# Attention followed by a gated feed-forward: k and v with nine tokens of two heads per partition, k-z-v in 64-row halves, the norm weight by a product, wo queued behind the weights

## The chip, the cores and the metric

The kernel runs on one core of a Trainium2 chip. The metric is the device time of one execution in microseconds (us); medians, ranges and clocks come from several executions. The profile is of one execution, recorded by the hardware profiler: for the kernel before a further one, elsewhere one of those timed. Engines in it: PE is TensorE's matmuls, PEld its weight loads, DVE is VectorE, ACT is ScalarE, POOL is GpSimd, SP is SyncE. Matmul ends are modelled, so I read their starts.

## The reference

```python
# q, k, v: 8 batches x 8 heads x 576 tokens x 64, float32
def phi(x, c, s):
    r = np.maximum(x, 0.0)
    return np.concatenate([r * c, r * s], axis=-1)          # 64 -> 128 features
q_p, k_p = phi(q, cos_w, sin_w), phi(k, cos_w, sin_w)       # angle = pi/2 * token / 576
kv  = np.einsum('bhsf,bhsd->bhfd', k_p, v)
z   = np.sum(k_p, axis=2)
num = np.einsum('bhsf,bhfd->bhsd', q_p, kv)
den = np.einsum('bhsf,bhf->bhs', q_p, z)[..., None] + 1e-06
x   = (num / den)                                           # then 4608 rows of 512
xn  = x / np.sqrt(np.mean(x * x, -1, keepdims=True) + 1e-06) * rms_g
g, val = xn @ w_gate, xn @ w_val                            # 512 -> 1536
out = (silu(g) * val) @ w_out                               # 1536 -> 512
```

The product of phi(k) with v, and with a column of ones for z, is called k-z-v here. It is needed once in each batch.

## The kernel before

Each batch has 576 tokens. Before, 512 of them lie four to a partition, and a tail of 64 is loaded and cast apart. A head's k-z-v is five matmuls of 128 rows that accumulate.

```python
def load_main(which, src, b, heads=(0, 8), bufs=one, queue=nc.sync):
    ...
        in_=src[b, h0:h1, 0:512, :].rearrange("h (p j) d -> p h (j d)", j=4),
...
def kvz_pe(b, pst, heads=range(8)):
    o = headview(pst)
    for h in heads:
        for c in range(5):
            lhsT = kp_main[b][:, c, h, :] if c < 4 else kpt[b % 2][:, h % 4, :]
            rhs = vvm[b % 2][:, c, h, :] if c < 4 else vvt[b % 2][:, h, :]
            nc.tensor.matmul(o[:, h // 4, h % 4, :], lhsT=lhsT, rhs=rhs,
                             start=(c == 0), stop=(c == 4))
```

The opening keeps TensorE busy with matmuls on a tile of zeros ("fillers") until the first data is there. `V` and `A` are VectorE and ScalarE; `q_tr_pe` is a transpose of phi(q) on TensorE, and `q_tr_evac` is its copy out.

```python
nc.sync.dma_start(out=gb[:, :], in_=moe_rms_g ... .to_broadcast([P, DM]))   # norm weight
...
filler(31, idle)
...                                 # phi(k) of batch 0
for c in (0, 1):
    q_phi(V, 0, c, 0)
    q_phi(A, 0, c, 1)
q_tr_pe(0, 0, psV[0][:, :])
filler(2, idle)
q_tr_evac(V, 0, 0, psV[0][:, :])
q_tr_pe(0, 1, psO[0][:, :])
filler(4, idle)
...                                 # k-z-v of batch 0
```

At the joint, k-z-v of batch 1 and the transposes of its q stand between the output matmuls of block 0.

```python
for n in range(NNT - 2):
    if n == 0:
        ...                         # phi(q) of batch 1, second half
    if n == 3:
        kvz_pe(1, psA)
        ...
    if 1 <= n <= 4:
        c = n - 1
        q_tr_pe(1, c, qbank[c])
        q_tr_evac(V if c < 2 else A, 1, c, qbank[c])
    if n == 2:
        v_cast(A, 1, LOW)
        v_cast(V, 1, HIGH)
    ...
    for j in range(4):
        out_mm(0, j, n, banks0[j])
```

Of the kernel before, what the change touches and what calls it, by code (L numbers as in the profile page):

```python
# [13 lines left out]
SYNC_DEP = mybir.DependencyInfo(mybir.DependencyClass.Sync, mybir.DependencyReason.DATA)  # L14

# [7 lines left out]
def kernel(  # L23
# [40 lines left out]
    LOW, HIGH = (0, 4), (4, 8)  # L64
# [4 lines left out]
    def load_main(which, src, b, heads=(0, 8), bufs=one, queue=nc.sync):  # L69
        key = (which, b)  # L70
        if key not in raw:
            raw[key] = bufs.tile([P, H, 4 * D], FP32, name=f"r{which}", tag=f"r{which}")
        h0, h1 = heads
        return queue.dma_start(
            out=raw[key][:, h0:h1, :],
            in_=src[b, h0:h1, 0:512, :].rearrange("h (p j) d -> p h (j d)", j=4),
        )

    def load_tail(which, src, b, queue=nc.sync):
        t = (four if which == "q" else two).tile(  # L80
            [P, 4, D], FP32, name=f"r{which}t", tag=f"r{which}t"
        )
        raw[(which + "t", b)] = t
        for g in range(2):
            d = queue.dma_start(
                out=t[64 * g : 64 * g + 64, :, :],
                in_=src[b, 4 * g : 4 * g + 4, 512:576, :].rearrange("h s d -> s h d"),
            )
        return d

    src_of = {"k": k, "q": q, "v": v}
    last_load = {}

    def load_piece(which, b, p):
        if p < 4:
            load_main(
                which, src_of[which], b, (2 * p, 2 * p + 2), two if which == "k" else one
            )
        else:
            load_tail(which, src_of[which], b)  # L100

    def load(which, b):
        load_main(which, src_of[which], b, bufs=two if which == "k" else one)
        last_load[(which, b)] = load_tail(which, src_of[which], b)

    def load_tokens(which, b, j0, j1):

        key = (which, b)
        if key not in raw:
            raw[key] = one.tile([P, H, 4 * D], FP32, name=f"r{which}", tag=f"r{which}")  # L110
        view = src_of[which][b, :, 0:512, :].rearrange("h (p j) d -> p h j d", j=4)
        return nc.sync.dma_start(
            out=raw[key][:, :, j0 * D : j1 * D],
            in_=view[:, :, j0:j1, :].rearrange("p h j d -> p h (j d)"),
        )

    first = {}
    load_main("k", k, 0, LOW, two)
    load_tail("v", v, 0, A)
    load_main("k", k, 0, HIGH, two)  # L120
    load_tail("k", k, 0, A)
    load_tokens("q", 0, 0, 2)
    first["v"] = load_main("v", v, 0, LOW)
    load_main("v", v, 0, (4, 7))
    load_main("v", v, 0, (7, 8))
    load_tokens("q", 0, 2, 4)
    nc.scalar.preload_act_table(AF.Silu)

    gb = one.tile([P, DM], FP32, name="gb")
    with nc.allow_non_contiguous_dma(reason="rms_g to all partitions"):  # L130
        nc.sync.dma_start(
            out=gb[:, :],
            in_=moe_rms_g.rearrange("(o d) -> o d", o=1).to_broadcast([P, DM]),
        )


    iota_i = one.tile([P, 2], mybir.dt.int32, name="iota_i")
    nc.gpsimd.iota(iota_i[:, :], pattern=[[0, 2]], base=0, channel_multiplier=1)
# [7 lines left out]
    fidx = one.tile([P, 1], FP32, name="fidx")  # L146
    th = one.tile([P, 10], FP32, name="th")
    tab = one.tile([P, 10], FP32, name="tab")
    ang = math.pi / 2.0 / float(S)
    nc.vector.tensor_copy(out=fidx[:, :], in_=iota_i[:, 0:1])  # L150
    for j in range(4):
        nc.vector.tensor_scalar(
            out=th[:, j : j + 1], in0=fidx[:, :], scalar1=4.0 * ang, scalar2=j * ang,
            op0=ALU.mult, op1=ALU.add,
        )
    nc.vector.tensor_scalar(
        out=th[0:64, 4:5], in0=fidx[0:64, :], scalar1=512.0, scalar2=ang,
        op0=ALU.add, op1=ALU.mult,
    )
    nc.vector.tensor_scalar(  # L160
        out=th[64:128, 4:5], in0=fidx[64:128, :], scalar1=448.0, scalar2=ang,
        op0=ALU.add, op1=ALU.mult,
    )
    nc.vector.tensor_scalar(
        out=th[:, 5:10], in0=th[:, 0:5], scalar1=math.pi / 2.0, scalar2=math.pi,
# [4 lines left out]
    def sin_of(c, lo=0, hi=P):  # L170
        return tab[lo:hi, c : c + 1]

    def cos_of(c, lo=0, hi=P):
        return tab[lo:hi, 5 + c : 6 + c]
# [5 lines left out]
    kpt = [one.tile([P, 4, F], BF16, name=f"kpt{i}") for i in range(2)]  # L180
    vvt = [one.tile([P, H, E], BF16, name=f"vvt{i}") for i in range(2)]
    vvm = [one.tile([P, 4, H, E], BF16, name=f"vvm{i}") for i in range(2)]
# [3 lines left out]
    for i in range(2):  # L186
        nc.gpsimd.memset(vvt[i][64:128, 0:4, :], 0.0)
        nc.gpsimd.memset(vvt[i][0:64, 4:8, :], 0.0)
        nc.gpsimd.memset(vvt[i][0:64, 0:4, D:E], 1.0)
        nc.gpsimd.memset(vvt[i][64:128, 4:8, D:E], 1.0)  # L190
        nc.gpsimd.memset(vvm[i][:, :, :, D:E], 1.0)
# [16 lines left out]
    def view4(t, heads):  # L208
        return t[:, heads[0] : heads[1], :].rearrange("p h (j d) -> p h j d", d=D)
# [9 lines left out]
    def k_phi(eng, b, c, part, heads=(0, 8)):  # L219

        o = slice(0, D) if part == 0 else slice(D, F)
        f = cos_of if part == 0 else sin_of
        if c < 4:
            if b not in kp_main:
                kp_main[b] = one.tile([P, 4, H, F], BF16, name="kpm", tag="kpm")
            src = view4(raw[("k", b)], heads)[:, :, c, :]
            phi(eng, kp_main[b][:, c, heads[0] : heads[1], o], src, f(c))
        else:
            phi(eng, kpt[b % 2][:, :, o], raw[("kt", b)][:, :, :], f(4))

    def q_phi(eng, b, c, part, heads=(0, 8)):
# [6 lines left out]
        t = qp_tiles[(b, c)]  # L238
        if c < 4:
            src = view4(raw[("q", b)], heads)[:, :, c, :]  # L240
            phi(eng, t[:, heads[0] : heads[1], o], src, f(c))
        else:
            phi(eng, t[:, :, o], raw[("qt", b)][:, :, :], f(4))
# [32 lines left out]
    def v_cast(eng, b, heads=(0, 8)):  # L276
        copy(
            eng,
            vvm[b % 2][:, :, heads[0] : heads[1], 0:D],
            view4(raw[("v", b)], heads).rearrange("p h j d -> p j h d"),  # L280
        )

    def v_cast_tail(eng, b):
        for g in range(2):
            copy(
                eng,
                vvt[b % 2][64 * g : 64 * g + 64, 4 * g : 4 * g + 4, 0:D],
                raw[("vt", b)][64 * g : 64 * g + 64, :, :],
            )
# [4 lines left out]
    def kvz_pe(b, pst, heads=range(8)):  # L294
        o = headview(pst)
        for h in heads:
            for c in range(5):
                lhsT = kp_main[b][:, c, h, :] if c < 4 else kpt[b % 2][:, h % 4, :]
                rhs = vvm[b % 2][:, c, h, :] if c < 4 else vvt[b % 2][:, h, :]
                nc.tensor.matmul(  # L300
                    o[:, h // 4, h % 4, :], lhsT=lhsT, rhs=rhs, start=(c == 0), stop=(c == 4)
                )

    def kvz_evac(eng, b, pst, bank):
        kvzs[(b, bank)] = three.tile([P, 4 * E], BF16, name="kvzs", tag=f"kvzs{bank}")
        copy(eng, kvzs[(b, bank)][:, :], pst[:, bank, 0 : 4 * E])

    def kvz_half(b, view, heads):
        o = view[:, 0, 0 : 4 * E].rearrange("p (h e) -> p h e", e=E)
        for h in heads:  # L310
            for c in range(5):
                lhsT = kp_main[b][:, c, h, :] if c < 4 else kpt[b % 2][:, h % 4, :]
                rhs = vvm[b % 2][:, c, h, :] if c < 4 else vvt[b % 2][:, h, :]
                nc.tensor.matmul(
                    o[:, h % 4, :], lhsT=lhsT, rhs=rhs, start=(c == 0), stop=(c == 4)
                )

    def kvz_half_evac(eng, b, view, bank):
        kvzs[(b, bank)] = three.tile([P, 4 * E], BF16, name="kvzs", tag=f"kvzs{bank}")
        copy(eng, kvzs[(b, bank)][:, :], view[:, 0, 0 : 4 * E])  # L320

    def nd_pe(b, j, pst):

        o = headview(pst)
        for h in range(H):
            g, i = h // 4, h % 4
            if j < 4:
                nc.tensor.matmul(  # L328
                    o[:, g, i, :], lhsT=qpT[(b, 0)][:, h, j * P : (j + 1) * P],
                    rhs=kvzs[(b, g)][:, i * E : (i + 1) * E], start=True, stop=True,  # L330
                )
            else:
                for bb in (b - 1, b):
# [4 lines left out]
                        rhs=kvzs[(bb, g)][:, i * E : (i + 1) * E], start=True, stop=True,  # L338
                    )

    def nd_half(b, j, g, bank):
        o = bank[:, 0 : 4 * E].rearrange("p (h e) -> p h e", e=E)
        for i in range(4):
            nc.tensor.matmul(
                o[:, i, :], lhsT=qpT[(b, 0)][:, 4 * g + i, j * P : (j + 1) * P],
                rhs=kvzs[(b, g)][:, i * E : (i + 1) * E], start=True, stop=True,
# [142 lines left out]
    filler(31, idle)  # L489
    for heads in (LOW, HIGH):  # L490
        for c in range(4):
            k_phi(V, 0, c, 0, heads)
            k_phi(A if heads is LOW or c < 2 else V, 0, c, 1, heads)
# [377 lines left out]
```

## Time and profile before

| | before |
|---|---|
| time, three runs | 329.54 us median (328.85 to 329.59) |
| TensorE busy | 320.2 us, 98% of the span |
| VectorE, ScalarE, GpSimd busy | 55%, 51%, 12% |
| k-z-v of a batch in TensorE's chain | 1.21 us (1.29 in batch 1) |
| first q transpose / k-z-v of batch 0 starts | 10.96 / 13.15 us |
| first 512-column gate product of block 0 starts | 32.15 us |
| k-z-v of batch 1 starts | 46.66 us |

The way to read it: TensorE bounds the kernel, so a change counts only where it alters TensorE's own work or a moment at which TensorE waits. The starts in the table are those of the first matmul of the kind. The chain of waits dates the same groups 0.16 us later, because there a piece begins only where the piece before it is taken to end; so 46.82 in the prediction and 46.66 here are the same matmul.

### The profile page before, as it was taken

The numbers are of one execution on the slowest core, as the hardware profiler recorded it, in microseconds if no ns is written. First come the engines' busy times: TensorE is split into PE (matmuls) and PEld (weight loads), VectorE is DVE, ScalarE is ACT, GpSimd is POOL, SyncE is SP. The second block draws the span as 40 slices with busy tenths as digits, with TensorE's granted clock in tenths as the row PEclk, the third lists the DMA queues.
The fourth block names the chain that finished last, engine by engine and source line by source line (L and its number), as shares of the span: only waits on it lengthen the run. The fifth ranks groups of instructions, "written<-read, shape, count | busy, mean of one in ns | idle before, by whom it ended". The sixth has DMA issues, their size and how long they took to land.

```text
span 327.8 us, 5943 instructions
## 1 busy us (share of the span) xinstructions
PE 320.2 (98%) x2189; PEld 163.3 (50%) x2189; DVE 181.6 (55%) x376; ACT 168.5 (51%) x326; POOL 37.8 (12%) x83
## 2 busy tenths in 40 slices
PE   8999999999999999999999999999999999999995
PEld 3568455654445444544454445444544444444443
DVE  3775667777745775677257745772577134203410
ACT  4565665876646556545664566455644233223321
POOL 3520032001200112012001120120011000000000
PEclk9999999999999999999999999999999999999999
DMA  7999999999599988967698669866621400020014
GB/s 208 280 196 250 275 214 270 304 223 209 133 249 220 174 209 242 224 173 166 208 181 213 170 190 181 218 172 208 135 55 32 130 33 0 19 111 0 0 34 97
DMA packets 95117, 54.14 MB, mean 165 GB/s; under 512 B 60016, under 2 KB 90480, under 8 KB 95088
## 3 DMA queue, kind: packets, MB, share of 16 engines
q1 hardware_dynamic: 89072, 48.65, 59.3%
q0 software_dynamic: 4768, 4.72, 8.9%
q10 hardware_dynamic: 1248, 0.39, 0.6%
q8 instruction: 17, 0.28, 0.4%
q14 instruction: 12, 0.10, 0.1%
HBM read 38.01 MB, written 9.44 MB: 145 GB/s over the span
## 4 chain that ended last, share of the span: by engine, by line
PE 93%; DMA 3%; DVE 2%; issue 1%; ACT 0%; SPq 0%; DVEq 0%
PE psG L444 27%; PE psV L444 27%; PE psC L464 26%; PE psA L300 3%; DMA rq<-in_q_dram 3%; PE psA L328 2%; PE psG L464 1%; PE psG L569 1%; PE psV L569 1%; PE psO L569 1%; PE psV L263 1%; PE psG L484 1%; PE psO L263 1%; PE psA L335 0%; PE psG L831 0%
## 5 line engine op out<-in xcount | busy, mean ns | idle before, releaser
L459 DVE TENSOR_TENSOR hT<-psV,sg 128x512 bf16<-128x512 f32 x102 | 70.4, 690 | 97.7 <-PE psV L444 86.3
L453 ACT ACTIVATE sg<-psG 128x512 f32<-128x512 f32 x102 | 60.6, 594 | 66.3 <-PE psG L444 66.2
L444 PE MATMUL psG<-xnT,wg 128*128 128x512 bf16 (+1 forms) x368 | 92.8, 374 | 0.2
L444 PE MATMUL psV<-xnT,wv 128*128 128x512 bf16 (+1 forms) x368 | 92.8, 375 | 0.0
L464 PE MATMUL psC<-wo,hT 128*128 128x512 bf16 x396 | 89.6, 379 | 0.0
L444 PEld LDWEIGHTS <-wv 128*128 128x128 bf16 x416 | 40.6, 98 | 47.4
L464 PEld LDWEIGHTS <-hT 128*128 128x128 bf16 x420 | 40.1, 98 | 46.5
L444 PEld LDWEIGHTS <-wg 128*128 128x128 bf16 x416 | 38.5, 97 | 41.4 <-issue 0.6
L272 ACT COPY osb<-psC 128x512 f32<-128x512 f32 (+1 forms) x33 | 19.1, 578 | 44.3 <-PE psC L464 43.6
L398 POOL TENSOR_TENSOR rs<-ms,mhalf 128x1 f32<-128x1 f32 x36 | 19.8, 549 | 184.6 <-ACT scr L393 184.6
L405 DVE SCALAR_TENSOR_TENSOR xn<-xt,rs,gb 128x512 bf16<-128x512 f32 x36 | 27.3, 757 | 14.1 <-POOL rs L398 14.0
L393 ACT ACTIVATE scr<-xt 128x513 bf16<-128x513 f32 x36 | 22.8, 635 | 23.4 <-DVE xt L382 22.5
L382 DVE TENSOR_TENSOR xt<-psA,rec 128x512 f32<-128x512 f32 x35 | 24.2, 691 | 1.2
L213 ACT ACTIVATE qp<-rq,tab 128x512 bf16<-128x512 f32 x32 | 22.3, 713 | 3.6 <-DMA rq<-in_q_dram 3.6
L213 ACT ACTIVATE kpm<-rk,tab 128x512 bf16<-128x512 f32 (+1 forms) x34 | 21.2, 675 | 0.5 <-DMA rk<-in_k_dram 0.5
L215 DVE TENSOR_SCALAR kpm<-rk,tab 128x512 bf16<-128x512 f32 (+1 forms) x38 | 15.3, 455 | 4.3 <-ACT tab L168 3.3
L215 DVE TENSOR_SCALAR qp<-rq,tab 128x512 bf16<-128x512 f32 x32 | 15.0, 480 | 2.5 <-DMA rq<-in_q_dram 2.5
L484 PE MATMUL psG<-warm 128*128 128x512 bf16 x49 | 14.1, 434 | 1.2 <-DVE fidx L150 1.2
L328 PEld LDWEIGHTS <-qpT 128*128 128x128 bf16 x248 | 11.7, 98 | 6.8 <-DMA qpT<-qp 0.5
L328 PE MATMUL psA<-kvzs,qpT 128*128 128x65 bf16 x248 | 12.9, 194 | 0.2
L444 PE MATMUL psV<-xnt_tail,wv 128*128 128x512 bf16 x48 | 12.3, 379 | 0.0
L444 PE MATMUL psG<-xnt_tail,wg 128*128 128x512 bf16 x48 | 12.3, 379 | 0.0
(95 smaller groups left out, 194.5 us busy)
## 6 DMA issues: line engine op xcount, KB each, us to landing
out_dram<-osb SPq DMA_DIRECT2D x32, 256.0 KB, 2.6
rk<-in_k_dram SPq DMA_DIRECT2D x20, 256.0 KB, 3.8
rv<-in_v_dram SPq DMA_DIRECT2D x20, 256.0 KB, 3.1
rq<-in_q_dram SPq DMA_DIRECT2D x20, 256.0 KB, 3.2
rk<-in_k_dram SPq DMA_DIRECT2D x2, 1024.0 KB, 8.7
rq<-in_q_dram SPq DMA_DIRECT2D x2, 1024.0 KB, 11.0
rv<-in_v_dram SPq DMA_DIRECT2D x3, 512.0 KB, 10.8
wo<-in_moe_w_out_dram POOLq DMA_DIRECT2D x4, 384.0 KB, 7.7
```

The lines of the kernel that those rows point to most:

```text
L213: nc.scalar.activation(out=out_ap, in_=in_ap, func=AF.Relu, scale=scale)
L215: eng.tensor_scalar(out=out_ap, in0=in_ap, scalar1=scale, scalar2=0.0, op0=ALU.mult, op1=ALU.max)
L272: nc.scalar.copy(out=o, in_=i)
L328: nc.tensor.matmul(o[:, g, i, :], lhsT=qpT[(b, 0)][:, h, j * P : (j + 1) * P], rhs=kvzs[(b, g)][:, i * E : (i + 1) * E], start=True, stop= ...
L382: nc.vector.tensor_tensor(out=xt[:, 0:DM].rearrange("p (b h d) -> p b h d", b=2, d=D), in0=o[:, :, :, 0:D], in1=rec[:, :, :].unsqueeze(3). ...
L393: nc.scalar.activation(out=scr[:, :], in_=xt[:, 0 : DM + 1], func=AF.Square, scale=1.0 / math.sqrt(DM), accum_out=ms[:, :],)
L398: nc.gpsimd.tensor_tensor(out=rs[:, :], in0=ms[:, :], in1=mhalf[:, :], op=ALU.pow)
L405: nc.vector.scalar_tensor_tensor(out=xn[:, :], in0=x_of[(b, j)][:, 0:DM], scalar=rs_of[(b, j)][:, :], in1=gb[:, :], op0=ALU.mult, op1=ALU. ...
L444: nc.tensor.matmul(pst[bank][:, cols[0] : cols[1]], lhsT=w[:, t, n * P : (n + 1) * P], rhs=x[:, t, cols[0] : cols[1]], start=(t == 0), sto ...
L453: nc.scalar.activation(out=sg[:, :], in_=psG[bank][:, :], func=AF.Silu)
L459: nc.vector.tensor_tensor(out=hTs[blk][:, n, :], in0=psV[bank][:, :], in1=sg[:, :], op=ALU.mult)
L464: nc.tensor.matmul(bank, lhsT=hTs[blk][:, n, j * P : (j + 1) * P], rhs=wo[:, n, :], start=(n == 0), stop=(n == NNT - 1),)
```

## The change

It is meant to do four things. First, k and v are loaded in runs of 2304 bytes, nine tokens to a partition, with two heads in the two halves of the partitions; the tails of k and v go. Second, k-z-v then contracts over 64 rows, in nine steps for each head, with the two heads in turn, so that the halves of the array may work side by side. Third, the norm weight is spread over the partitions by a one-row product, and not by a broadcast load. Fourth, wo's first slice is queued directly behind the other weights, and the transposes of the joint are begun one step earlier.

```diff
+            in_=src[b, 2 * r0 : 2 * r1, :, :]
+            .rearrange("h s d -> (h s d)")
+            .rearrange("(r p n) -> p r n", p=P, n=NJ * D),
...
+    def kvz_mm(b, banks, rs=(0, 4)):
+        for r in range(*rs):
+            for j in range(NJ):
+                for c in range(2):
+                    lo = 64 * c
+                    nc.tensor.matmul(
+                        banks[c][:, r * E : (r + 1) * E],
+                        lhsT=kp_main[b][lo : lo + 64, j, r, :],
+                        rhs=vvm[b % 2][lo : lo + 64, r, j, :],
+                        start=(j == 0), stop=(j == NJ - 1),
+                    )
...
-    filler(31, idle)
+    filler(30, idle)
...
+    wo_load(0)
...
     q_tr_pe(0, 0, psV[0][:, :])
-    filler(2, idle)
     q_tr_evac(V, 0, 0, psV[0][:, :])
+    nc.tensor.matmul(psO[1][:, :], lhsT=ones[:, :], rhs=g_row[:, :], start=True, stop=True)
     q_tr_pe(0, 1, psO[0][:, :])
-    filler(4, idle)
+    filler(1, idle)
...
     for n in range(NNT - 2):
+        if n == 3:
+            kvz_pe(1, psA)
...
+        if n in (0, 1, 2, 4):
+            c = min(n, 3)
+            q_tr_pe(1, c, qbank[c])
+            q_tr_evac(V if c < 2 else A, 1, c, qbank[c])
         if n == 0:
...
+        if n == 2:
+            v_cast(A, 1, *LOW)
+            v_cast(V, 1, *HIGH)
         if n == 3:
-            kvz_pe(1, psA)
...
-        if 1 <= n <= 4:
-            c = n - 1
...
-        if n == 2:
-            v_cast(A, 1, LOW)
-            v_cast(V, 1, HIGH)
```

## The prediction

> **What bounds the kernel now.** I read the page first: which engine is full, then whether the chain agrees.
>
> ```profile
> PE 320.2 (98%) x2189; PEld 163.3 (50%) x2189; DVE 181.6 (55%) x376; ACT 168.5 (51%) x326; POOL 37.8 (12%) x83
> ...
> PE 93%; DMA 3%; DVE 2%; issue 1%; ACT 0%; SPq 0%; DVEq 0%
> ```
>
> TensorE is 98% busy and 93% of the chain that ended last is TensorE work. VectorE and ScalarE are half idle, so work moved between them costs nothing where they keep up. I then went through the starts of the matmuls in the trace and listed every place where the next start comes later than the stream's pace (216 ns at 512 columns, 30 ns at 65). From 62 us to the end there are only two waits, 0.30 and 0.20 us. So only three places can move the time: the opening up to about 24 us, the joint between batches 0 and 1 at 42 to 61 us, and the TensorE time of k-z-v, once in each batch.
>
> The third, in the chain in order of time (start us, us, what), and a precedent for half-array matmuls in the timeline (start us, us, engine, line, operation):
>
> ```profile
> 46.82 1.29 PE psA L300 x40
> ...
> 69.72 1.21 PE psA L300 x40
> ```
> ```profile
> 118.81 0.38 PE L464 MATMUL psC<-wo,hT 128*128 128x512 bf16 x1
> ...
> 119.12 0.33 PEld L335 LDWEIGHTS <-qtT 128*64 128x64 bf16 x16 [0.42 <-issue]
> 119.12 0.45 PE L335 MATMUL psA<-kvzs,qtT 128*64 128x65 bf16 x16
> ...
> 119.50 0.39 PE L464 MATMUL psC<-wo,hT 128*128 128x512 bf16 x1
> ```
>
> k-z-v costs 1.21 us for 40 matmuls, 30 ns each, all on the path. The L335 matmuls alternate between two 64-column halves of the array. In the trace their starts come in pairs 3 to 5 ns apart, a pair every 25 to 48 ns, mostly about 30; and the first start comes 94 ns late, the next full-array matmul after them 97 ns late: entering and leaving the split costs 0.19 us.
>
> The opening, from the same timeline:
>
> ```profile
> 3.63 1.28 ACT L127 ACT_TABLE_LOAD   x1 [3.63 <-issue]
> ...
> 5.21 1.71 ACT L213 ACTIVATE kpm<-rk,tab 128x256 bf16<-128x256 f32 x4
> 5.22 1.14 DVE L215 TENSOR_SCALAR kpm<-rk,tab 128x256 bf16<-128x256 f32 x4 [3.28 <-ACT tab L168]
> ...
> 10.18 1.33 ACT L213 ACTIVATE qp<-rq,tab 128x512 bf16<-128x512 f32 x2 [1.17 <-DMA rq<-in_q_dram]
> ...
> 10.96 0.62 PE L263 MATMUL psV<-ident,qp 128*128 128x128 bf16 x8 [0.66 <-ACT qp L213]
> ```
>
> TensorE runs fillers until q lands at 10.16 us and ScalarE has made its half of phi(q). And the joint:
>
> ```profile
> 44.04 0.61 PE L263 MATMUL psV<-ident,qp 128*128 128x128 bf16 x8 [0.51 <-DVE qp L215]
> ...
> 44.78 1.03 ACT L272 CAST vvm<-rv 128x1024 bf16<-128x1024 f32 x1
> ...
> 48.59 1.01 ACT L272 COPY qpT<-psV 128x1024 bf16<-128x1024 bf16 x1
> ```
>
> Here TensorE loses 0.67 us to a late phi(q). The cast of v comes well before k-z-v, and the copy of the third transpose comes after it.
>
> **What the Trainium skill says.** "TensorE: Matmul & The Clock Gate", Part 3, says that matmuls in different row groups run concurrently, starting about 4 ns apart. The trace shows this for column halves; no run yet shows it for row halves. "TensorEngine Tiling (Array Packing)", Key Properties, says that a change of tiling mode drains the engine: the 94 and 97 ns agree. The first page, Part 1, also gives a floor of about 25 ns from start to start for small matmuls; the 3 to 5 ns inside pairs show that it doesn't hold between halves. "DMA: Bandwidth & Descriptors", Specifications, puts line rate at 512 B and above; the trace is less simple. In the opening a 256 B packet took 18 to 24 ns, a 512 B one 28 to 38 and a 1024 B one mostly 48 to 65, so about 11 ns seem to be fixed for each packet.
>
> **The change, part by part.**
>
> *k-z-v.* 40 matmuls of 128 rows become 72 of 64 rows, in an order that alternates the halves: 36 pairs. With 31 ns a pair (estimate, from the L335 pairs) and 0.19 us of switching: 36 x 0.031 + 0.19 = 1.31 us against 1.21. Batches 1 to 7 pay that on the path: 7 x 0.10 = +0.7 us. Half the contraction rows bring no saving, since a pair takes the time of one full matmul, 36 is nearly 40, and the switch eats the difference.
>
> *phi(k) and casts.* Each batch has 18 pieces of 128x256 in place of 8 of 128x512 and 2 of 128x256. From start to start the trace has ScalarE at 0.40 us for 256 columns and 0.62 for 512, VectorE at 0.26 and 0.40. So ScalarE pays 9 x 0.40 = 3.6 us instead of 4 x 0.62 + 0.40 = 2.9, VectorE 2.4 instead of 1.9. With blocks of over 30 us and both engines half idle, this lies beside TensorE's work, except at the joint. GpSimd's tail casts vanish, off the path.
>
> *Opening.* The tails of k and v (256 B packets) and the 256 KB broadcast of the norm weight go; k and v come in 2304 B runs. By the packet fit, 11 ns plus 43 ns per KB, such a packet takes about 108 ns, some 340 GB/s over 16 engines, against about 290 now (estimate). k (1.18 MB) and half of q (0.52 MB at about 240 GB/s), starting at 2.2 us, should have been sent by about 8.1 and landed by about 9.0, against 10.16. The angle table is no longer late, as ScalarE's queue holds one DMA ahead of the table load instead of four. But ScalarE now has 15 pieces of 128x128, about 0.30 us each by extrapolation: from 5.05 to 9.6 us. Its phi(q) then runs to 10.3, so the first transpose starts near 10.35, not 10.96: 0.6 us. Then come a product in fp32 for the norm weight (four passes assumed, 0.9 us, in place of two fillers), the second transposes, and k-z-v at about 12.4 instead of 13.15. v should land 0.6 to 0.9 us earlier. The four copies of k-z-v and the 0.59 us copy of the norm weight on ScalarE take back a little. The first normalised tile should be about 0.85 us earlier. The weights, now gated by an earlier v and freed from the broadcast, should come early enough: -0.85 us.
>
> *Joint.* In the new order the third q transpose stands before k-z-v, with its copy on ScalarE, ahead of the cast of v there. Let E be the end of batch 0's gate and value products (42.68 before). ScalarE's 9 pieces of phi(k) push its gate activations to about E+0.3. phi(q) of the first quarter is ready at E+0.4 (VectorE), so 0.4 us of stall stays. Transposes of 0.45 and output groups of 0.87 alternate, with a small wait for the third: its transposes end at about E+3.45. Then ScalarE copies (1.01) and casts v (1.03 x 1152/1024 = 1.16), in sequence: k-z-v can start at about E+5.65. Before it started at E+4.14 with one transpose group less, 0.45 us, ahead of it. Net +1.05 us, a wait that takes the place of the one that the earlier phi(q) was to remove. It is mostly ScalarE's 2.2 us against one output group of 0.87 on TensorE.
>
> *wo behind the weights* only reorders transfers. wo's first slice landed at 41.63, in time before, and will now land earlier: nothing gained directly.
>
> Sum: 0.7 - 0.85 + 1.05 = +0.9, so about 330.4; I put 330.3, as the joint's +1.05 hangs on several estimates that could each shrink it.
>
> **Rivals.** (a) Row halves don't pair, because both halves' weight loads serialise. Then 72 matmuls at about 29 ns make 2.1 us with no switch, 2.3 with it: +0.9 to +1.1 a batch, about +7 us, 337. Against it: the L335 pairs, whose weight loads pair too (16 in 0.33 us). For it: those load 64 columns each, these 128. One chance in ten; a partial loss (40 ns a pair, +0.4 a batch, 333) one in seven. (b) The joint doesn't stall, because ScalarE's queue runs ahead of what I reckon: then 329.3, or 328.6 if the old 0.67 us goes as well. (c) The weights bound the opening: value weights landed at 19.41, 24.46 and 32.42 and were wanted about 0.5, 0.2 and 0.7 us later, so an opening 0.85 us faster gains only what they gain. If they gain nothing, 331. (d) Smaller DMA load helps the steady part: at most the 0.20 us wait for a transposed q.
>
> **Range and chances.** Opening and joint each have an error of about 0.8 us; k-z-v runs from -0.5 to +3. So 327.9 to 333.8 eight times in ten. Two per cent is 6.6 us: no place holds so much to gain (all of TensorE's waits after 10 us come to about 4.5 us), so faster 0.02; slower needs rival (a) in full, 0.06.
>
> **What would show it.** In the changed profile: k-z-v of x72 in about 1.3 us in the chain, starts in pairs some 4 ns apart; the first q transpose near 10.35 after ScalarE's phi(q); the full gate products starting near 31.5 instead of 32.31; and before k-z-v of batch 1 a TensorE wait of about 1.5 us that names ScalarE's cast of v. I am wrong if k-z-v takes 1.7 us or more, if no wait stands there, or if the opening's first product waits for a weight transfer.

## The result, and the profile after

| four runs each, same rounds | median, us | range, us |
|---|---|---|
| before | 329.56 | 328.85 to 330.22 |
| after | 331.23 | 330.9 to 331.86 |

The ratio is 1.0053, with a 95% interval of 1.0027 to 1.0079. A ratio is the mean time of one kernel's fast runs over the mean of the other's fast runs of the same rounds, so it is not quite the ratio of the medians. The changed kernel is slower by about 1.7 us, which is the same within 2%. All runs were at granted clocks of 0.998 to 1.0.

**The page and the chain.** TensorE has 1.4 us more of busy time in 252 more instructions, and still carries 92% of the chain.

```profile
PE 321.6 (98%) x2441; PEld 162.9 (49%) x2441; DVE 186.3 (57%) x411; ACT 175.9 (53%) x365; POOL 28.9 (9%) x63
...
PE 92%; ACT 3%; DVE 2%; issue 1%
```

The chain in order of time (start us, us, what): k-z-v of batch 1, then of batch 3 with the gate product behind it.

```profile
48.44 1.33 PE psA L281 x72
...
101.71 1.26 PE psA L281 x72
102.97 0.97 PE psG L425 x4
```

The chain's 1.26 us leaves out part of the price. The gate product behind k-z-v takes 0.97 us here, where the same four matmuls take 0.86 elsewhere in this chain: the rest is the exit from the split array. From the starts in the trace, batch 3 has 36 pairs whose two matmuls start 3 to 4 ns apart, a pair every 32.5 ns on average. The first pair starts 96 ns late, and the next full matmul starts 126 ns after the last pair, so 94 ns late. That makes 36 x 0.0325 + 0.096 + 0.094 = 1.36 us, against 1.21 before.

**The landmarks.** I took the start of the same matmul in both traces and looked for where the difference changes. All values are us, of one execution each.

| start of | before | after | difference |
|---|---|---|---|
| first q transpose | 10.96 | 10.63 | -0.33 |
| first full gate product of block 0 | 32.15 | 32.13 | -0.02 |
| k-z-v of batch 1 | 46.66 | 48.44 | +1.78 |
| first 512-column gate product of block 1 | 62.65 | 63.93 | +1.28 |
| outputs of block 1 | 81.89 | 83.55 | +1.66 |
| gate products of block 2 | 93.28 | 94.64 | +1.36 |
| outputs of block 2 | 116.18 | 117.47 | +1.29 |
| outputs of block 3 | 150.22 | 151.64 | +1.42 |
| last outputs | 313.27 | 315.07 | +1.80 |

So the opening gained nothing, the joint lost 1.30, batch 2 in block 1 lost 0.38, and the later blocks lost about 0.13 for each k-z-v. Against that, the kernel before waited 0.30 us just ahead of 93.28 and 0.20 at 108.76, and the changed one did neither. The +1.78 at k-z-v of batch 1 holds 0.45 for the third group of transposes, which now stands ahead of it and not behind; the next landmark shows the net value.

**The opening.** The data came earlier, as intended. Windows of the two traces from 2 to 5 us (stretch, length, then busy us and count of PE, PEld, DVE, ACT, POOL, then the granted clock, the DMA share and GB/s), before and after:

```profile
2.00:5.00 3.00, 3.00 (x8) 1.03 (x7) 0.00 (x0) 1.35 (x2) 1.72 (x14) 1.00 1.00 294
```
```profile
2.00:5.00 3.00, 3.00 (x8) 1.06 (x7) 0.94 (x6) 1.46 (x5) 0.09 (x6) 1.00 1.00 364
```

The rate is 364 GB/s where it was 294. k landed at 4.25 and 5.75 us (5.12 and 7.35 before), the first half of q at 8.84 (10.16), the first slices of the weights at 15.01 and 17.52 (16.84 and 19.41). Now the timeline (start us, us, engine, line, operation, idle time before it and what ended it), first the fillers of before, then the opening of after:

```profile
1.19 9.11 PE L484 MATMUL psG<-warm 128*128 128x512 bf16 x31 [1.19 <-DVE fidx L150]
```
```profile
1.19 9.61 PE L465 MATMUL psG<-warm 128*128 128x512 bf16 x30 [1.19 <-DVE warm L144]
...
8.86 1.34 ACT L208 ACTIVATE qp<-rq,tab 128x512 bf16<-128x512 f32 x2
...
10.63 0.61 PE L253 MATMUL psV<-ident,qp 128*128 128x128 bf16 x8
...
11.17 1.12 PE L505 MATMUL psO<-g_row,ones 1*128 1x512 f32 x2
```

phi(q) for the first transposes was ready at 9.59 us, but the transposes have no bracket: TensorE was not idle ahead of them. It was still running fillers, to 10.80. Thirty fillers last longer here than 31 did before, because 14 of them ran at half clock (427 ns from start to start and not 216), against 11 before. How many do so differs from execution to execution: the profiles have 7 to 14. The kernel before would not have noticed: with 14 slow ones its 31 fillers would end at 1.19 + 14 x 0.427 + 17 x 0.216 = 10.84, still ahead of its first transpose at 10.96.

**The joint**, timeline of after, with the same columns:

```profile
43.05 0.61 PE L253 MATMUL psV<-ident,qp 128*128 128x128 bf16 x8 [0.40 <-DVE qp L210]
...
46.32 1.01 ACT L262 COPY qpT<-psV 128x1024 bf16<-128x1024 bf16 x1 [1.60 <-PE psV L253]
...
47.23 1.16 ACT L262 CAST vvm<-rv 128x1152 bf16<-128x1152 f32 x1
...
48.44 1.33 PE L281 MATMUL psA<-vvm,kpm 64*128 64x65 bf16 x72 [1.30 <-ACT vvm L262]
```

ScalarE stood idle for 1.60 us until the third transposes gave it something to copy, and only then cast v, which had landed at 40.37. Its queue is in order, and the copy stood first. By starts, TensorE came 1.46 us late to k-z-v (the bracket's 1.30 counts from the modelled end of the matmul before).

**Batch 2**, timeline of after: k-z-v begins, and stops inside for the second half of v, which VectorE casts too late.

```profile
70.93 1.58 PE L281 MATMUL psA<-vvm,kpm 64*128 64x65 bf16 x72
70.96 0.75 DVE L264 CAST vvm<-rv 128x1152 bf16<-128x1152 f32 x1
```

The group takes 1.58 us and not 1.33: 0.25 us of waiting that the kernel before did not have.

### The profile page after: what moved, and what is told of

Same layout as the page of the kernel before. It is cut to its first block, busy times and chain, and to the rows that moved or that the text cites. A ratio compares the mean times of both kernels' runs of the same rounds, so it can differ in the third digit from the quotient of the medians.

```text
span 329.4 us, 6432 instructions
## 1 busy us (share of the span) xinstructions
PE 321.6 (98%) x2441; PEld 162.9 (49%) x2441; DVE 186.3 (57%) x411; ACT 175.9 (53%) x365; POOL 28.9 (9%) x63
## 4 chain that ended last, share of the span: by engine, by line
PE 92%; ACT 3%; DVE 2%; issue 1%
PE psC L445 26%; PE psG L425 25%; PE psV L425 24%; PE psG L465 3%; PE psA L281 3%; PE psA L309 2%; ACT kpm L208 2%; PE psG L445 1%; PE psG L552 1%; PE psV L552 1%; PE psO L552 1%; ACT sg L434 1%; PE psV L253 1%; DVE hT L440 1%; PE psO L253 1%
## 5 line engine op out<-in xcount | busy, mean ns | idle before, releaser
L208 ACT ACTIVATE kpm<-rk,tab 128x256 bf16<-128x256 f32 (+1 forms) x78 | 31.7, 478 | 1.5 <-DMA rk<-in_k_dram 1.5
L210 DVE TENSOR_SCALAR kpm<-rk,tab 128x256 bf16<-128x256 f32 (+1 forms) x84 | 22.5, 336 | 2.0 <-DMA rk<-in_k_dram 2.0
L465 PE MATMUL psG<-warm 128*128 128x512 bf16 x43 | 13.4, 463 | 1.2 <-DVE warm L144 1.2
```

Of the source, the lines that this page charges most:

```text
L208: nc.scalar.activation(out=out_ap, in_=in_ap, func=AF.Relu, scale=scale)
L210: eng.tensor_scalar(out=out_ap, in0=in_ap, scalar1=scale, scalar2=0.0, op0=ALU.mult, op1=ALU.max)
L465: nc.tensor.matmul(bank, lhsT=warm[:, 0:P], rhs=warm[:, :], start=True, stop=True)
```

## The experiments

The theory: the joint's order on ScalarE costs 1.3 to 1.4 us; the gain of the opening is eaten by fillers whose number is fixed; k-z-v costs 0.15 us more a batch, because the halves do pair. The rivals: the joint's loss lies elsewhere (in phi(q), or in DMA); the fillers are harmless; the small parts (norm weight, wo) carry the loss. Eleven kernels ran, and all gave correct results. The kernel before ran again, at medians of 329.27 (e1 to e4), 329.27 (e5 to e8) and 329.19 us (e9 to e11). Unless said otherwise, an edit is on the changed kernel.

### e1: the cast of v ahead of the third transposes

```diff
+        if n == 2:
+            v_cast(A, 1, *LOW)
+            v_cast(V, 1, *HIGH)
         if n in (0, 1, 2, 4):
             c = min(n, 3)
             q_tr_pe(1, c, qbank[c])
...
-        if n == 2:
-            v_cast(A, 1, *LOW)
-            v_cast(V, 1, *HIGH)
```

> The changed kernel with one move: at the joint the two casts of v stand ahead of the third q transpose and its copy, instead of behind them. Theory (ScalarE's queue order makes the 1.46 us wait before k-z-v of batch 1): the wait falls under 0.2 us, k-z-v starts near 47.0 instead of 48.44, and the time falls by 1.2 to 1.5 us, to about the time of the kernel before (ratio 0.998 to 1.003). Rival (ScalarE is simply late at the joint from its nine pieces of phi(k) and the phi(q) behind them): the wait only moves, less than 0.5 us is gained.

Measured: 329.56 us (329.13 to 330.01, four runs), ratio 1.0016 (0.9999 to 1.0033). Its timeline:

```profile
43.93 1.15 ACT L262 CAST vvm<-rv 128x1152 bf16<-128x1152 f32 x1
...
45.64 1.01 ACT L262 COPY qpT<-psV 128x1024 bf16<-128x1024 bf16 x1 [0.56 <-PE psV L253]
...
46.40 1.34 PE L281 MATMUL psA<-vvm,kpm 64*128 64x65 bf16 x72
```

The cast fills ScalarE's idle time, and k-z-v starts without a bracket; the 0.10 us that its start comes late is the entry to the split. k-z-v starts 2.04 us earlier than in the changed kernel. Of this, 0.68 is an earlier opening of this execution (full gate product at 31.45 and not 32.13, with 11 slow fillers and not 14, in unchanged code); the remaining 1.36 is the wait. The joint's loss is the order of two instructions in ScalarE's queue, and this run shows it.

### e2: 24 fillers for 30

```diff
-    filler(30, idle)
+    filler(24, idle)
```

> The changed kernel with 24 fillers at the start instead of 30. Theory (in the opening TensorE itself is the bound: its fillers end at 10.8 us, though phi(q) is ready at about 9.6): the first q transpose starts at 9.6 to 9.8, the full gate products about 1.0 to 1.4 us earlier than 32.29, the time falls by as much. Rival (casts of v on VectorE, the fp32 product and the four copies set the opening, whatever the fillers do): 0.3 us or less is gained.

Measured: 330.54 us (330.1 to 332.26, four runs), ratio 1.0051 (1.0021 to 1.008). Its timeline:

```profile
9.59 0.62 PE L253 MATMUL psV<-ident,qp 128*128 128x128 bf16 x8 [0.72 <-ACT qp L208]
```

The first transpose now waits for phi(q), as the bracket says. The full gate product starts at 31.09, so 1.04 us earlier than in the changed kernel; the wait at the joint is still 1.46. The time does not show the theory's 1.0 to 1.4 us: the ratio is hardly below the changed kernel's 1.0053. Three things blur it: the changed kernel's opening differs between executions (e1 had it 0.68 us earlier with the same code); e2's profile has two waits for a transposed q, 0.12 us at 105 and 0.38 at 110, which the changed kernel's has not; and one of the four runs, the 332.26, had a clock of 0.993. The trace supports the theory; the time is inconclusive.

### e3: the halves one after the other

```diff
         for r in range(*rs):
-            for j in range(NJ):
-                for c in range(2):
+            for c in range(2):
+                for j in range(NJ):
                     lo = 64 * c
```

> The changed kernel with the 64-row matmuls of k-z-v in another order: nine of the upper half, then nine of the lower, so that neighbours use the same half. Theory (the alternating halves run at the same time, 32 ns a pair): without pairs 72 matmuls at about 29 ns make 2.1 us and 0.2 of switching, 2.3 instead of 1.36 us, over 7 batches +6 to +7 us, ratio about 1.025. Rival (the pairing brings nothing, 64-row matmuls are just short): no change.

Measured: 333.53 us (333.66 and 333.4), ratio 1.0132 (1.0111 to 1.0152). The chain of e3, k-z-v of a later batch:

```profile
136.57 1.65 PE psA L281 x72
```

With the way in it is 1.75 us, against 1.36: 0.39 more in each batch, 2.7 in seven. The time grew by 2.3 against the changed kernel. So the order in pairs is worth having, but both expectations missed. The theory said 6 to 7 us, as if only one half worked at a time; in fact 72 of them take (1.75 - 0.19) / 72 = 21.7 ns each on average, if the switching costs what it does in the changed kernel. Batch 0 shows why, as its first half writes to psG and its second to psV (timeline):

```profile
11.99 0.36 PE L281 MATMUL psG<-vvm,kpm 64*128 64x65 bf16 x6
12.18 0.20 PE L281 MATMUL psV<-vvm,kpm 64*128 64x65 bf16 x1
12.20 0.19 PE L281 MATMUL psG<-vvm,kpm 64*128 64x65 bf16 x1
12.21 0.20 PE L281 MATMUL psV<-vvm,kpm 64*128 64x65 bf16 x1
12.23 0.19 PE L281 MATMUL psG<-vvm,kpm 64*128 64x65 bf16 x1
```

Within one half, starts are mostly 32 to 33 ns apart (29 to 39 in a run of nine). But the next nine, in the other half, begin when only six of these nine have started. So the runs overlap by three matmuls at each end, and the starts that lie 15 to 18 ns apart belong to different halves. This edit therefore took away a part of the pairing, not all of it.

### e4: the norm weight and wo alone, on the kernel before

```diff
+    nc.scalar.dma_start(out=g_row[:, :], in_=moe_rms_g.rearrange("(o d) -> o d", o=1))
...
-        nc.sync.dma_start(out=gb[:, :], in_=moe_rms_g ... .to_broadcast([P, DM]))
...
+    wo_load(0)                                           # straight behind the weights
...
     q_tr_pe(0, 0, psV[0][:, :])
-    filler(2, idle)
     q_tr_evac(V, 0, 0, psV[0][:, :])
+    nc.tensor.matmul(psO[1][:, :], lhsT=ones[:, :], rhs=g_row[:, :], start=True, stop=True)
...
+    copy(A, gb[:, :], psO[1][:, :])
```

> The kernel before with the two small parts of the change alone: norm weight by an fp32 product behind the first q transposes in place of two fillers and of the broadcast load, and the first slice of wo queued behind the weights; k and v and the order of the joint as before. Theory (these parts do not carry the loss): between -0.3 and +0.7 us, the product of about 1.05 us costing up to 0.6 us in TensorE's queue in the opening, the joint unchanged. Rival (the early wo takes bandwidth from q of batch 1 and makes the joint late): over 1 us slower, with a longer wait for phi(q) near 44 us.

Measured: 329.71 us (329.1 to 330.22, four runs), ratio 1.0015 (0.9996 to 1.0035). The full gate product starts at 32.43 us (32.15 before), and the wait at the joint is 0.64, like the 0.67 of before. The two small parts do not carry the loss: they may cost about 0.3 us in the opening, and nothing after it.

### e5: the cast first, and phi(q) of the first quarters ahead of part of phi(k)

```diff
-    for j in range(NJ):
-        at(0, 8 + j // 5, "post", k_phi, V, 1, j, 0)     # and ScalarE's half
     for c in range(2):
-        at(0, 10 + c, "post", q_phi, V, 1, c, 0)
+        at(0, 9, "post", q_phi, V, 1, c, 0)
+    for j in range(NJ):
+        n = 8 if j < 5 else 10 + (j - 5) // 2
+        at(0, n, "post", k_phi, V, 1, j, 0)
...             # and the edit of e1
```

> The kernel with the cast first, and phi(q) of the first two quarters of batch 1 put ahead of the last four of its nine phi(k) pieces on ScalarE and VectorE. Theory (the 0.57 us wait before the first q transpose of the joint, 0.57 in the run with the cast first too, is ScalarE's and VectorE's backlog of phi(k) pieces): that wait falls under 0.15 us, and the time is 0.3 to 0.6 us below the run with the cast first, ratio to before about 1.000. Rival (q of batch 1 lands too late, or the phi(k) pieces come late for k-z-v instead): the wait stays, or a new one of like size stands before k-z-v.

Measured: 329.09 us (328.52 to 329.62, four runs), ratio 0.9992 (0.9975 to 1.0009). Its timeline:

```profile
39.13 1.33 ACT L208 ACTIVATE qp<-rq,tab 128x512 bf16<-128x512 f32 x2 [0.28 <-DMA rq<-in_q_dram]
...
41.73 0.61 PE L253 MATMUL psV<-ident,qp 128*128 128x128 bf16 x8
```

The wait at the first transposes falls from 0.57 us to 0.09. A new one of 0.27 arises at the third, where VectorE's phi(q) is now late. The kernel is 2.1 us faster than the changed one and level with the one before.

### e6: 36 fillers for 30

```diff
-    filler(30, idle)
+    filler(36, idle)
```

> The changed kernel with 36 fillers instead of 30. Theory (TensorE's own fillers bound the opening of the changed kernel): six more fillers at 0.216 us put off the first q transpose, and everything behind it, by close to 1.3 us: ratio to before about 1.009, 0.9 to 1.3 us above the changed kernel. Rival (a wait elsewhere sets the opening and the fillers only fill it): at most 0.3 us slower than the changed kernel.

Measured: 332.0 us (331.49 to 332.92, four runs), ratio 1.0084 (1.0064 to 1.0103). Its timeline:

```profile
1.19 9.95 PE L465 MATMUL psG<-warm 128*128 128x512 bf16 x36 [1.19 <-DVE warm L144]
...
10.97 0.61 PE L253 MATMUL psV<-ident,qp 128*128 128x128 bf16 x8
```

The transposes start as the fillers end, without a bracket, although only 10 of the 36 were slow in this execution. The time is above the changed kernel's by 0.8 us between the medians and by 1.0 between the ratios, which is the better measure as the two ran in different calls. That is about the low end of the theory's 0.9 to 1.3 and beyond the rival's 0.3, though the intervals of the two ratios overlap. Fillers are on the path. With e2's trace, this is what shows the step on the opening to be wrong.

### e7: the joint of e5, 24 fillers, and v of batch 2 cast one step earlier

```diff
+    filler(24, idle)                                     # for 30
...
-        vb, vn = (b, 3) if late else (b - 1, 14)
+        vb, vn = (b, 2) if late else (b - 1, 14)
...             # and the edits of e5
```

> The reordered joint, 24 fillers, and the casts of v of batch 2 one step earlier (the trace of the changed kernel has a 0.25 us wait for one of them inside k-z-v). Theory: opening and joint gain independently, so against the reordered joint alone another 0.4 to 1.0 us for the fillers and 0.25 for the cast: ratio to before 0.995 to 0.998, faster than both kernels. Rival (weights, or wo, arrive too late for an earlier TensorE): no more than 0.3 us below the reordered joint, with a wait that names a weight transfer.

Measured: 330.05 us (328.59 to 331.17, six runs), ratio 1.0013 (0.9988 to 1.0038). The wait in batch 2 is gone, but the spread is 2.6 us where e5's is 1.1, and it goes with the granted clock: 328.59, 329.04 and 329.53 us at 1.0, 0.999 and 0.998, 330.59, 330.57 and 331.17 at 0.995, 0.989 and 0.988. The theory's ratio was missed, and no wait for weights as in the rival explains it. TensorE's timeline in its profile (the 330.59), and windows with the columns as above:

```profile
1.19 7.00 PE L465 MATMUL psG<-warm 128*128 128x512 bf16 x24 [1.19 <-DVE warm L144]
9.64 0.62 PE L253 MATMUL psV<-ident,qp 128*128 128x128 bf16 x8 [1.45 <-ACT qp L208]
...
11.98 0.63 PE L465 MATMUL psG<-warm 128*128 128x512 bf16 x1
```
```profile
8.00:11.00 3.00, 1.55 (x11) 0.74 (x10) 2.20 (x8) 2.88 (x8) 0.58 (x1) 1.00 1.07 370
11.00:15.00 4.00, 4.00 (x83) 2.72 (x82) 2.00 (x3) 1.54 (x4) 4.00 (x6) 0.57 1.15 171
```

From 11 to 15 us the clock is 0.57: TensorE went back to half speed from 11.4 to 14.8. It had been idle for 1.45 us, then had transposes and the one-row product.

### e8: as e7, with the product among the fillers

```diff
+    filler(14, idle)                                     # for 24
+    nc.tensor.matmul(psO[1][:, :], lhsT=ones[:, :], rhs=g_row[:, :], start=True, stop=True)
+    filler(6, idle)
...
     q_tr_evac(V, 0, 0, psV[0][:, :])
-    nc.tensor.matmul(psO[1][:, :], lhsT=ones[:, :], rhs=g_row[:, :], start=True, stop=True)
```

> The kernel of the last description with the fp32 product for the norm weight moved from behind the first q transposes into the row of fillers (14 before it, 6 after it). Theory (the product's 1.05 us lie on the path between the first and the second q transposes): 0.2 to 0.8 us faster, the second transposes starting right after phi(q)'s second quarter at about 10.2 us. Rival (the casts of v on VectorE set the start of k-z-v anyway, so the product is hidden): 0.2 us or less.

Measured: 328.37 us (327.85 to 329.39, six runs), ratio 0.9973 (0.9956 to 0.9991), all clocks 0.997 to 1.0. Its timeline, and its window from 11 to 15 us:

```profile
5.80 1.12 PE L471 MATMUL psO<-g_row,ones 1*128 1x512 f32 x2
...
9.79 0.62 PE L253 MATMUL psV<-ident,qp 128*128 128x128 bf16 x8 [1.46 <-ACT qp L208]
...
10.40 0.62 PE L253 MATMUL psO<-ident,qp 128*128 128x128 bf16 x8
```
```profile
11.00:15.00 4.00, 3.84 (x96) 2.50 (x95) 3.41 (x10) 2.75 (x8) 4.00 (x6) 1.00 0.99 159
```

The product now lies in time that TensorE spends waiting anyway, the second transposes follow the first, and k-z-v of batch 0 starts at 11.23 us and not 12.99, but then stops for 0.31 us for a cast of v on VectorE, the engine that the rival named. The clock stays full, after the same idle time as in e7. The gain on e7, 1.7 us, is more than the theory's 0.2 to 0.8, because e7 had lost time to its clock. This is the only kernel with an interval clear of 1 on the fast side: it beats the kernel before by 0.9 us, and the changed one by 2.6 to 2.9 (ratios, medians). Its lead over e5 is within both intervals, and in its profile the full gate product starts at 31.30 us, like e5's 31.28; so I do not claim that moving the product is itself what gains.

### e9: as e8, with eleven fillers behind the product

```diff
-    filler(6, idle)
+    filler(11, idle)
```

> The kernel with the product among the fillers, with five more fillers behind it (14 before, 11 after). With 20, TensorE stood idle for 1.46 us before the first q transpose in the profiled run. Theory (some idle time there is harmless as long as the clock does not fall, but more fillers than phi(q) needs cost time): between 0.3 us faster, if the clock fell in some runs with 20, and 0.4 us slower, if the fillers now last beyond 9.7 us in the runs that warm up late. Rival (the gain of that kernel came from the shorter row of fillers alone): 0.6 to 1.1 us slower.

Measured: 328.74 us (327.76 to 329.96, six runs), ratio 0.9974 (0.9945 to 1.0002). It cannot be told from e8. The full gate product starts at 30.65 us in its profile, the earliest of all.

### e10: as e5, with v of batch 2 cast one step earlier, and 30 fillers

```diff
-        vb, vn = (b, 3) if late else (b - 1, 14)
+        vb, vn = (b, 2) if late else (b - 1, 14)
...             # and the edits of e5
```

> The reordered joint with all 30 fillers and the casts of v of batch 2 one step earlier: the kernel that came out at ratio 1.0013, but with the 30 fillers of the changed kernel instead of 24. Theory (with 24 the clock is halved for 3.4 us in some runs, and that cost more than the earlier start gained): ratio 0.997 to 0.999, with the granted clock of every run at 0.997 or more. Rival (the earlier casts of v did the harm): ratio 1.000 or more.

Measured: 329.49 us (328.06 to 329.89, six runs), ratio 0.9988 (0.9959 to 1.0016), clocks 0.998 to 1.0. The clock is sound with 30 fillers, so e7's trouble does not come from the earlier cast. Whether the cast itself gains its 0.25 us can't be read here: the profile has a wait of 0.87 us for a transposed q that comes by DMA, near 104 to 112 us. That wait was 0.20 in the kernel before and 0.22 to 0.89 in e2, e3, e5, e7, e8 and e10; in the profiles of after, e1, e4, e6, e9 and e11 there is none. I found no order in this.

### e11: as e8, with six fillers ahead of the product

```diff
-    filler(14, idle)
+    filler(6, idle)
```

> The kernel with the product among the fillers, with eight fillers fewer (6 before it, 6 after). Theory (TensorE's clock is halved after a stretch of little work, and the opening then runs at half speed): TensorE is idle for about 3 us before the first q transpose, the clock in the profile falls to half at some point before 15 us, the mean granted clock is near 0.99, and the time is 0.7 to 2 us above that of the kernel with 20. Rival (idle TensorE costs nothing while it waits for q): the same time within 0.3 us, clock 0.997 or more.

Measured: 328.56 us (327.63 to 329.15, four runs), ratio 0.9963 (0.9924 to 1.0001), clocks 0.999 to 1.0. The kernel was not slower, so the rival's number holds. But the theory was hardly tested: all 12 fillers and the product ran at half clock and lasted to 8.4 us, so TensorE waited for 1.2 us by its bracket, not about 3, before the first transpose at 9.79. The clock rose late, at 9.3 us, and stayed up.

## Why the prediction was right or wrong

The time was 331.23 us against 330.3 predicted, inside the range, and within 2% of before as held most likely. The mechanisms were mostly right. One term of the sum failed, one was mis-sized, and one small wait was not seen. In place of 0.7 - 0.85 + 1.05 = +0.9, the landmarks give -0.02 (opening) + 1.30 (joint) + 0.38 (block 1 with batch 2) - 0.37 (block 2, where waits of 0.30 and 0.20 us of before are gone) + 0.51 (from there to the last outputs) = +1.80, and the spans differ by 1.6. That the sum came within 0.9 of this is in part luck: those 0.50 us, for which no cause is shown, came off the total.

**Opening: the step that failed is "Its phi(q) then runs to 10.3, so the first transpose starts near 10.35".** The packets did what the fit said: q landed at 8.84 us, said 9.0 (the prediction's own figures put the end of the sending at 7.85 us, not 8.1). phi(q) for the first transposes was even ready at 9.59. But the step let the first transposes start when their data was ready, and never worked out when the 30 fillers ahead of them end. Before, they ended first, so the data set the start; with earlier data the fillers did, at 10.80. The first transpose came at 10.63 by its start and the gate product gained 0.02, not 0.85. The loss of the gain is not the same in each execution: five profiles of this opening with 30 fillers and the product behind the transposes (after, e1, e3, e5, e10) have the full gate product at 32.13, 31.45, 31.62, 31.28 and 32.12, so -0.43 on average against 32.15. The average is a rough one, as these kernels differ elsewhere (e3 in k-z-v, which the opening has too). In e3 and e5, with 8 slow fillers, the row ended first, and the first transpose waited 0.35 and 0.42 us for phi(q). e2 (-1.06 with fewer fillers) shows that the gain was there to be had, and e6 that fillers cost it.

The fillers are only the first part of this miss of 0.83 us. The first transpose came 0.28 later than predicted; the other 0.55 lie behind it. From there to the full gate product the prediction had about 20.95 us (-0.85 at the end, -0.6 at the start), the kernel before took 21.19, and the changed one 21.50, as did e1, e2, e5, e6 and e10 (21.49 to 21.51). So this stretch grew by 0.31 where it was to shrink by 0.24: 0.17 up to k-z-v of batch 0, 0.14 behind its start. The product took 1.05 us for 0.9, and k-z-v enters and leaves the split twice there; how the 0.31 is made up, no run isolates.

**k-z-v: right in kind, +0.15 us and not +0.10 a batch.** The rows' halves do pair, 3 to 4 ns apart. The switching cost 0.19 us as said; a pair took 32.5 ns and not 31, and 36 times 1.5 ns are the missing 0.05. The prediction misread its precedent here: its 25 to 48 ns run from the second matmul of a pair to the next pair. From pair to pair the L335 starts are 30 to 52 ns apart, mostly 30 to 34. Rival (a) is refuted by the trace of after. Its price was not measured, since the halves still overlap in e3; 72 starts at 33 ns would make 2.4 us before switching (an estimate from e3).

**Joint: the mechanism was right, and the size was off by 0.3.** The wait that was to name ScalarE's cast of v is there, with 1.46 us for "about 1.5". With E at 42.49, k-z-v started at E + 5.95 for E + 5.65 predicted. 0.17 of the 0.30 is the stall at the first transposes, 0.57 and not 0.4. The rest comes from the 0.20 between the end of the third transposes, 46.12 us by their starts, and the start of their copy on ScalarE at 46.32, for which the prediction had nothing; some 0.1 of it was won back, as the cast started 0.91 us after the copy and not 1.01. Net that is 5.95 - 4.15 - 0.45 = +1.35. Undone in e1, it gave 1.36 back. Rival (b) fell.

**phi(k) and casts "beside TensorE's work, except at the joint": wrong once.** In batch 2, VectorE's cast of v stopped k-z-v for 0.25 us. e7 removed that wait by casting one step earlier.

**Weights and wo: right.** They came early enough (the last value weights at 30.59 us and not 32.42, wo's first slice at 34.46 and not 41.63), and no product of the changed kernel's opening waited for them. Rival (c) played no part, though in e8, with an opening faster still, TensorE waits 0.20 us by its starts for a value weight that landed at 23.77.

**Rival (d), lighter DMA in the steady part: not shown.** The 0.20 us wait for a transposed q in the kernel before is absent after, but such waits come and go between the profiles of all kernels (e10). The 0.30 us ahead of the gate products at 93.28, for which the profile names no cause, stand in the profile of before alone.

**Left open:** why e7's clock fell. Three of its six runs show it, the profiled one among them, perhaps also the one slow-clocked run of e2; both have 24 fillers and the product behind the first transposes. Idle time alone does not explain it, as e8 was idle for as long. What fits the traces is the whole stretch between the first row of fillers and the next filler, just ahead of k-z-v. In e7's profile it lasts from the end of the row at 8.03 us to the fall at 11.38, 3.35 us with nothing but idle time, transposes and the one-row product; in the other profiles it is 3.0 us at most (2.9 in e2, 2.7 in e8, 2.5 in e11, 2.1 in after). The Trainium skill, "TensorE: Matmul & The Clock Gate", Part 1, says that the clock falls after an idle window of about 3.4 us, in windows that run freely. The trace agrees: e7's clock rose at 4.56, fell at 11.38 and rose again at 14.80, so 2 x 3.41 and 3.42 us apart. That transposes and a one-row product count as idle there, no run here isolates. Part 1 also says that the number of slow first matmuls varies from run to run; it did, from 7 to 14, and fewer slow ones end the fillers sooner and make the stretch longer (8 in e7's profile, 11 in e2's).

## What to carry to other kernels

When data comes earlier, ask what else stands in front of its first use: padding of a fixed length, such as warm-up matmuls, becomes the bound as soon as the data beats it. Its duration need not be fixed: the same 30 fillers lasted 8.1 us in e3's profile and 9.4 in after's. On an engine with an in-order queue, put the instruction whose data is already there (here the cast of v) ahead of the one that must wait for another engine (the copy of a transpose); that order alone was worth 1.4 us. Splitting a contraction into halves that run in pairs doesn't make it cheaper when the number of pairs hardly falls, and entering and leaving the split together cost 0.19 us each time.

## What the Trainium skill lacked or had wrong

- "TensorE: Matmul & The Clock Gate", Part 1, gives a floor of about 25 ns from start to start. It does not hold between the row halves of a pair (3 to 4 ns in the trace of after, which agrees with Part 3). Within one half it held: 29 to 39 ns in e3.
- "TensorEngine Tiling (Array Packing)", Key Properties, says that a change of tiling mode drains the engine, but not for how long. Row halves cost 96 ns on the way in and 94 on the way out; the column halves of this kernel cost 94 and 97.
- I found no page that gives a time for a float32 product: one row by 128 by 512 took 1.05 us from its start to the next matmul's, in two records of the trace of after.
- "DMA: Bandwidth & Descriptors" gives no time for one packet at the sizes of this kernel: in the opening, 256 and 1024 bytes took about 20 and 56 ns (before), 512 bytes 28 to 35 (before and after) and 2304 bytes about 99 (after).
